# A decode block, forward and backward, on one core: the next step's key tile between two value tiles, a new order of every engine, and output rows in four column groups of TensorE

## Chip, core and metric

The kernel runs on one core of one Trainium2 chip. The core has five engines with their own instruction streams (TensorE, called PE; VectorE, DVE; ScalarE, ACT; GpSimd, POOL; SyncE, SP, which here only issues transfers) and 16 DMA engines that move data between HBM and the on-chip memory. The metric is the device time of one execution in microseconds, the median of several.

## What is computed

The reference computes a decode block with one new position per batch and then its whole gradient, for B = 2, D = 576, 32 query heads, 16 key heads, 4096 cached positions, head size 128 and a hidden size of 4608, all in bf16:

```python
xn = _layernorm(x)
y  = x + A(xn, k_cache, v_cache, wq, wo) + B(xn, w_gate, w_up, w_down)
# A: q = xn @ wq; p = softmax(q k^T / sqrt(128)); o = p v; o @ wo    (each key head serves two query heads)
# B: ((xn @ w_gate) * (xn @ w_up)) @ w_down
out, vjp = jax.vjp(f, x, k_cache, v_cache, wq, wo, w_gate, w_up, w_down)
return (out, *vjp(grad_out))
```

The outputs are out_0 (the block's output, 2 rows of 576), out_1 (the gradient of x, 2 rows), out_2 and out_3 (the gradients of the key and value cache, 2 x 16 x 4096 x 128 each), out_4 and out_5 (of wq and wo), out_6, out_7 and out_8 (of w_gate, w_up and w_down). The caches are read once (64 tiles of 1 MB) and gradients of the same size are written once (64 stores of 1 MB), and so are the weights: 92.48 MB in and 92.48 MB out.

## The kernel before

**Steps.** The attention goes in 16 steps s: eight groups of two key heads, for each of the two batches. A step loads two key tiles and two value tiles (128 x 4096 bf16, 1 MB, one for each head), and makes two 1 MB stores of dV (out_3, the softmax weights times the gradient of the head's output) and two of dK (out_2, the score gradients times q). The functions are `load_kv` (L1143) for the tiles, `softmax` (L1327), `dscore` (L1383), `contract` (L1434, products with a tile), and `head_outer` (L1287), whose matmuls L1299 build the blocks of dV and dK in PSUM. ACT (L470) or DVE (L472) copies each block of 128 x 1024 from PSUM into a bf16 tile, which is called an eviction here; after four of them `put` (L695) issues the store on SP (L699).

**Weights.** `load_w` (L1161) loads wq, wo, w_gate, w_up and w_down in between, and the MLP (`mlp`, L856) and the projections run among the attention's steps. The weights' gradients are outer products with few rows; `rows_outer`, `cols_outer`, `wide_outer` and `tail_outer` (L818) form them. `tail_outer` stores the last 64 rows of a gradient; some of these stores (the argument `few`) go out as 4 x 16 x 512 instead of 64 x 512.

**Buffers.** One ring of 16 tiles of 1 MB (`big`) serves key and value tiles, transposed tiles, gradients and weights, with a cap for each user. DVE transposes tiles at L466. SP issues 227 transfers between HBM and the on-chip memory (all but two small ones), in order, and each waits for the one eight before it.

**Who sets the order.** A class `Order` (L105 to L240) runs when the program is built. Each piece of the kernel is a generator that yields what it needs (an engine for so long, a buffer, a transfer, an event). The class keeps a model of when engines, buffers and transfers are free, and among the pieces that can go on an engine within `SLACK` of the first it picks the one of lowest priority value, `pr(name, s)` (L349): 28 for each step, and an offset from the tables `PR`, `HEAD`, `TAIL` and `OFF`. So the order of the instructions on every engine, SP included, is fixed in the program and comes out of these tables. `MLP_AT`, `WQ_AT` and `WO_AT` say when the weights are wanted.

**The last rows.** `final_out` (from L1502) adds x and the transposed sums to make out_0: two matmuls bring x (L1499), and 64-column matmuls with a unit matrix (L1513, L1516) add the sums, all on partitions 0 and 1. `final_dx` (from L1521) makes out_1: the norm's gradient on DVE (L1534 to L1545) and the same kind of transposing matmuls (L1549, L1552). In `rows_put` (L1489) ACT (L1491) and DVE (L1493) copy one part each into the tile `xy`, and SP stores it (L1495).

Of the kernel before, what the change touches and what calls it, by code (L numbers as in the profile page):

```python
# [104 lines left out]
class Order:  # L105
# [3 lines left out]
    def __init__(self):  # L109
        self.free = {e: 0.0 for e in ("PE", "ACT", "DVE", "POOL", "SP")}  # L110
        self.slots = {}
        self.home, self.cap, self.used = {}, {}, {}
        self.lines = Lines()
        self.quad, self.kind = (None, 0.0, 0.0), None
        self.streams = []
        self.count = 0
        self.log = []
        self.lanes = {"HW": [], "SW": []}
# [45 lines left out]
    def start(self, s):  # L164
# [30 lines left out]
    def run(self):  # L195
        while self.streams:
# [8 lines left out]
            if e is not None:  # L205
                t, _, s, e = min((c for c in cand if c[3] == e and c[0] <= t + SLACK[e]), key=lambda c: (c[1], c[0]))
# [27 lines left out]
            elif r[0] == "dma":  # L234
                self.free[e] = t + r[2]
# [55 lines left out]
def DMA(engine, cost, nbytes, row=8192):  # L291
    packet = 0.0364 * row + 8.7
    return ("dma", engine, cost, 0.02 + nbytes / 16e3 * packet / row, packet)

NBIG, NWW, NBD = 16, 5, 3
CAP = {"G": 2, "X": 10, "kv": 6, "st": 5}
OFF = {"turn0": {0: -1015.2, 1: -14.6, 2: -608.5, 3: -352.4, 4: -44.2, 5: -609.4, 6: 1026.5, 7: -575.3, 8: -336.9,
       9: -48.1, 10: 73.1, 12: 183.6, 13: 1140.9, 15: 354.0}, "turn1": {0: -158.8, 1: 373.8, 2: -399.3, 3: -123.5,  # L300
       4: -561.8, 5: 1792.7, 6: 184.6, 7: -225.4, 8: -1188.5, 9: -525.0, 10: -1211.4, 11: -134.5, 12: 1399.2, 13:
       -786.3, 14: 125.3, 15: -889.4}, "att": {0: -320.6, 1: 25.1, 2: -524.3, 3: 1437.6, 4: -1231.0, 5: 704.1, 6:
       -946.7, 7: -1656.2, 8: -1046.6, 9: 659.5, 10: -617.2, 11: -169.8, 12: 46.5, 13: -31.6, 14: -222.6, 15:
       1033.5}, "dsc": {0: -1811.3, 1: -9.9, 2: 131.1, 3: 301.3, 4: -3.2, 5: 235.2, 6: -975.3, 8: 26.8, 9: 229.2,
       10: -420.4, 11: 210.0, 12: 19.1, 13: 299.2, 14: 9.4}, "conv": {0: -2015.6, 1: 231.3, 2: -0.4, 3: -50.3, 4:
       -1165.8, 5: 1061.5, 6: 135.8, 7: 373.5, 8: -2359.6, 9: 3.5, 10: 1574.4, 11: 172.6, 12: 216.0, 13: 448.3, 14:
       255.6, 15: 10.6}, "con": {0: -32.2, 1: 1152.5, 2: 1696.5, 3: 720.8, 4: 638.1, 5: 104.8, 6: -260.9, 7: -158.3,
# [3 lines left out]
       9: -103.2, 10: -395.3, 11: 2850.9, 12: 125.0, 13: 2376.4, 15: -25.5}, "front": {0: -90.0, 1: 2844.9, 2:  # L311
       -805.5, 3: -966.7, 4: 1527.3, 5: 109.2, 6: 51.9, 7: -924.3, 8: -171.1, 9: -1466.9, 10: -796.2, 11: 95.0, 12:
       407.0, 13: 194.7, 14: 42.9, 15: -116.8}, "back": {0: -1180.5, 1: 591.1, 2: -2708.2, 3: 979.9, 4: 556.1, 5:
# [7 lines left out]
       13: -595.2, 14: -250.1, 15: 5.1}, "mlp": {0: 248.5, 1: 1168.1, 2: -620.3, 3: -398.1, 4: -321.8, 5: 2002.0, 6:  # L321
       162.1, 7: -3.7, 8: -33.1, 9: -2.4, 10: 1014.3, 11: 985.4, 12: 835.4, 13: -9.7, 14: 314.7, 15: -413.5},
       "load": {0: 1074.9, 1: -427.7, 2: 2940.0, 4: -302.0, 5: 501.3, 6: 157.2, 7: 2723.0, 8: 41.7, 9: 175.7, 10:
       -1207.2, 11: -514.7, 12: -5.8, 13: 248.9, 14: 607.8, 15: -253.7}, "wload": {0: -271.1, 1: 208.8, 2: -1828.2,
       3: 108.3, 4: 438.0, 5: -390.0, 6: 623.3, 7: 89.8, 8: -357.2, 9: -50.4, 10: 1806.6, 11: 48.4, 12: -1247.3, 13:
       3030.4, 14: 857.3, 15: 1037.7}, "mload": {0: 867.2, 1: -358.1, 2: -1319.2, 3: 100.2, 5: 58.5, 6: -3446.8, 9:
       -71.5, 10: -371.1, 11: -312.3, 12: 9.2, 13: 247.9, 14: 253.2, 15: -7.2}}
MLP_AT = [1.14, 5.4, 2.05, 2.45, 26.26, 69.69, 14.36, 0.0, 155.88]
WQ_AT = [-126, 9, 14, 22, -10, -36, 47, 13]
WO_AT = [-81, -88, -157, -95, 31, 1, -2, -56]  # L330
# [3 lines left out]
BIAS = 0.188  # L334
SLACK = {"PE": 0.06, "ACT": 0.25, "DVE": 0.4, "POOL": 10000.0, "SP": 10000.0}
STEP = 28.0
HEAD = {"turn0": -995.0, "turn1": -3790.2, "att": -3348.0, "dsc": 396.0, "conv": -832.5, "con": 1401.5, "out1":
        -1892.2, "out0": 2828.7, "front": 21.6, "back": 291.8, "W0": -1455.9, "W1": -155.0, "BD1": 1364.6, "BD0":
        2903.1, "mlp": 2389.4, "load": -3080.4, "wload": 394.7, "mload": -742.1}
TAIL = {"turn0": 3370.1, "turn1": 9221.8, "att": 665.4, "dsc": 359.0, "conv": 2694.5, "con": 2347.7, "out1": 7925.6,  # L340
        "out0": -1730.3, "front": 756.2, "back": 2986.8, "W0": 3398.4, "W1": -331.2, "BD1": -2581.8, "BD0": -508.7,
        "mlp": -5065.9, "load": 6824.2, "wload": 208.6, "mload": 3569.7}
PR = {"turn0": 1475.9, "turn1": 1614.7, "att": -4652.5, "dsc": -2890.4, "conv": 226.3, "con": -1413.1, "out1":
      3893.4, "out0": 2308.0, "front": 679.0, "back": 881.2, "W0": -1279.8, "W1": -624.6, "BD1": 2069.1, "BD0":
      -1551.4, "mlp": -735.6, "wout": -435.6, "store": -3305.7, "load": -1982.4, "wload": -3953.8, "fin": 5877.7,
      "const": 11595.3, "mload": -2275.6}
# [8 lines left out]
def kernel(  # L355
# [339 lines left out]
    def put(dst, src, nbytes, row, tag, slot, ready):  # L695
        yield WAIT(*ready)
        for d, x in zip(dst, src):
            yield DMA("SP", 0.36, nbytes, row)
# [119 lines left out]
    def tail_outer(rhss, dsts, p, event, w0=0, few=()):  # L818
# [5 lines left out]
        yield SPAWN(put(dsts, src, 64 * FS * 2, 1024, "tl", i, done), p + PR["store"])  # L824
# [31 lines left out]
    def mlp(i, hh, sl, Lgu, Ld, wd_slot):  # L856
# [36 lines left out]
        for k in range(NB):  # L893
            for e in range(2):
# [20 lines left out]
                               few=(0, 1) if i in FEW_M else (1,)), po)  # L915
# [136 lines left out]
    def group_back(g):  # L1052
# [13 lines left out]
        for t, x in ((0, R), (1, Q)):  # L1066
# [9 lines left out]
                               few=(0,) if g in FEW_G else ()), po)  # L1076
# [66 lines left out]
    def load_kv():  # L1143
        n = 0
        for s in range(NS):
            g, b = divmod(s, Bq)
            for t in range(2):
                for l in range(G):
                    yield PRIO(pr("load", s) if n else -1e5)
                    i = yield ACQ("kv")  # L1150
                    yield DMA("SP", 0.36, 1 << 20)
                    nc.sync.dma_start(kv_t[i][:], views[t][b, G * g + l])
                    kvS[s][t][l] = i
                    yield ("lset", kvL[s][t][l])
                    yield SET(issued[n])
                    n += 1
# [4 lines left out]
    def load_w(item):  # L1161
        kind, i = item
        if kind in ("wq", "wo"):
# [3 lines left out]
            if kind == "wq":  # L1167
# [5 lines left out]
                yield DMA("SP", 0.4, 128 * 4 * FS * 2, 1024)  # L1173
# [3 lines left out]
            else:  # L1177
                yield DMA("SP", 0.36, 128 * GH * D * 2, 4608)
# [3 lines left out]
        else:  # L1182
# [7 lines left out]
            for w, Wsrc in enumerate((B_w_gate, B_w_up)):  # L1190
                b = yield ACQ("G")
                sl["G"].append(b)
                yield DMA("SP", 0.4, 128 * 4 * width * 2, 2 * width)
# [9 lines left out]
            for hh, k in enumerate(ks):  # L1203
                d = yield ACQ("ww")
                Ld = Event()
                yield DMA("SP", 0.36, 128 * FC * D * 2, 4608)
# [282 lines left out]
    def rows_put(o, n, out):  # L1489
        yield ACT(0.4)  # L1490
        nc.scalar.copy(view(xy[:], 0, 2, n * D, [[P, 5], [1, 64]]), o[0:2, 0, 0:320].rearrange("p (k n) -> p k n", k=5))  # L1491
# [110 lines left out]
```

## Time and profile before

| | before |
|---|---|
| time, median of 3 runs | 463.32 us (462.25 to 463.77) |
| the profiled execution | 462.65 us, its span 460.7 us |
| mean granted TensorE clock | 0.721 |
| PE, DVE, ACT, POOL busy | 80%, 79%, 73%, 31% of the span |
| DMA | 185.97 MB, mean 404 GB/s |

The span is the time from the first to the last event of the execution in the profile; the execution's own time is some 2 us longer. The page cuts the span into 40 slices of 11.5 us and gives the busy share of each engine in tenths, and for the DMA engines the mean share of the 16 and the rate. Further views give the busy time in stretches of one's choice, the instructions of a stretch in order of time (the timeline), the chain of waits that ended last, and for each engine what its idle time ended with. SPq is SP's queue of transfers.

### The profile page before, as it was taken

How to read it: one execution, taken by the hardware profiler on the slowest of the kernel's cores; microseconds unless marked ns; L12 is line 12 of the kernel's file. 1: busy time of each engine (PE TensorE's matmuls, PEld its weight loads, DVE VectorE, ACT ScalarE, POOL GpSimd, SP SyncE). 2: the span in 40 equal slices, each digit the busy share in tenths (PEclk: the TensorE clock that was granted, in tenths of full speed). 3: DMA queues.
4: the chain of work that ended last, by engine and by line, in shares of the span. 5: the costliest groups of instructions: out<-in, count | busy, mean ns of one | idle time of the engine just before them, and what ended most of it. 6: DMA issues, size and time to landing. Idle time of an engine off the chain costs nothing.

```text
span 460.7 us, 15711 instructions
## 1 busy us (share of the span) xinstructions
PE 369.5 (80%) x6750; PEld 214.3 (47%) x6750; DVE 365.9 (79%) x708; ACT 336.8 (73%) x516; POOL 143.4 (31%) x174
## 2 busy tenths in 40 slices
PE   1688879798986786896978897877988887987994
PEld 1445456555443343554546364544444542544453
DVE  8887888896789687878887679886976987887782
ACT  4269638878986586775767859867867997897973
POOL 0740043403407341660016151050164364063000
PEclk9967676888776667757685678877567676675856
DMA  8999999999999999999999999999999999999995
GB/s 316 413 408 422 410 423 400 410 415 398 373 424 421 408 422 410 421 419 413 413 403 417 417 418 419 422 418 388 398 423 417 418 423 426 423 409 392 421 346 209
DMA packets 40494, 185.97 MB, mean 404 GB/s; under 512 B 3424, under 2 KB 12136, under 8 KB 24040
## 3 DMA queue, kind: packets, MB, share of 16 engines
q1 hardware_dynamic: 40416, 184.96, 99.0%
q8 instruction: 53, 0.87, 0.7%
q14 instruction: 17, 0.14, 0.1%
q10 hardware_dynamic: 8, 0.00, 0.0%
HBM read 92.48 MB, written 92.48 MB: 401 GB/s over the span
## 4 chain that ended last, share of the span: by engine, by line
DMA 34%; PE 30%; ACT 14%; DVE 12%; issue 5%; SPq 3%; DVEq 0%; ACTq 0%
DMA big<-in_A_v_cache_dram 15%; DMA out_dram<-big 14%; ACT big L470 12%; DVE big L466 7%; PE ps_o L1299 5%; PE ps_m L1451 4%; PE ps_o L730 4%; PE ps_m L1277 4%; DMA big<-in_A_k_cache_dram 3%; SPq L1201 2%; PE ps_o L767 2%; DVE big L472 2%; PE ps_m L895 2%; PE ps_m L681 2%; DMA ww<-in_A_wq_dram 1%
## 5 line engine op out<-in xcount | busy, mean ns | idle before, releaser
L470 ACT CAST big<-ps_o 128x1024 bf16<-128x1024 f32 (+2 forms) x309 | 278.9, 964 | 49.8 <-PE ps_o L1299 24.3
L466 DVE STREAM_TRANSPOSE big<-big 128x1024 f32<-128x1024 f32 x146 | 176.3, 1222 | 16.1 <-DMA big<-in_A_v_cache_dram 6.3
L1265 POOL TENSOR_TENSOR BD<-vr,mask 128x2048 bf16<-128x2048 bf16 x32 | 115.3, 3604 | 114.3 <-DVE vr L472 45.4
L472 DVE CAST big<-ps_o 128x1024 bf16<-128x1024 f32 (+1 forms) x69 | 73.4, 1065 | 19.4 <-PE ps_o L767 6.1
L1277 PE MATMUL ps_m<-big,W 128*32 128x128 bf16 x2048 | 59.7, 280 | 4.5 <-issue 1.7
L1242 POOL COPY W<-rep 32x16 bf16<-32x16 bf16 x128 | 24.8, 193 | 117.9 <-DVE rep L1015 102.0
L1277 PEld LDWEIGHTS <-W 128*32 128x32 bf16 x2048 | 47.2, 125 | 25.1 <-issue 23.9
L1299 PE MATMUL ps_o<-BD,dd 32*128 32x512 bf16 x256 | 46.9, 497 | 9.1 <-ACT big L470 8.1
L1299 PE MATMUL ps_o<-BD,pp 32*128 32x512 bf16 x256 | 44.6, 473 | 8.9 <-ACT big L470 7.3
L466 DVE STREAM_TRANSPOSE big<-ww 128x1152 f32<-128x1152 f32 (+1 forms) x25 | 32.9, 1318 | 2.6 <-DMA out_dram<-big 2.5
L1451 PE MATMUL ps_m<-big,pp 128*32 128x512 bf16 x256 | 28.9, 540 | 4.1 <-DVE pp L466 2.4
L1451 PE MATMUL ps_m<-big,dd 128*32 128x512 bf16 x256 | 27.8, 528 | 1.7 <-DVE dd L466 0.6
L1299 PEld LDWEIGHTS <-dd 32*128 32x128 bf16 x256 | 11.2, 98 | 26.5 <-issue 20.0
L1299 PEld LDWEIGHTS <-pp 32*128 32x128 bf16 x256 | 10.3, 95 | 28.1 <-issue 24.5
L767 PEld LDWEIGHTS <-xnr 32*128 32x128 bf16 x368 | 13.1, 114 | 14.5 <-issue 13.1
L730 PE MATMUL ps_o<-dyr,R 32*32 32x288 bf16 x256 | 17.8, 401 | 1.2 <-ACT big L470 1.1
L767 PE MATMUL ps_o<-D,xnr 32*128 32x128 bf16 x256 | 13.9, 265 | 5.7 <-ACT big L470 4.3
L730 PE MATMUL ps_o<-dyr,hb 32*32 32x288 bf16 x288 | 15.7, 328 | 2.8 <-ACT big L470 2.7
L1047 POOL COPY qr<-qd 128x256 bf16<-128x256 bf16 x8 | 3.2, 398 | 47.4 <-DVE qd L472 43.2
L895 PE MATMUL ps_m<-big,Wdy 128*128 128x128 bf16 x162 | 16.7, 285 | 0.6 <-DVE cr L1403 0.5
L895 PEld LDWEIGHTS <-Wdy 128*128 128x128 bf16 x162 | 15.1, 131 | 2.9 <-issue 2.7
L1352 ACT COPY mr<-m 1x128 f32<-1x128 f32 x16 | 4.7, 295 | 15.1 <-DVE m L1350 14.9
(210 smaller groups left out, 488.2 us busy)
## 6 DMA issues: line engine op xcount, KB each, us to landing
out_dram<-big SPq DMA_DIRECT2D x74, 1024.0 KB
big<-in_A_k_cache_dram SPq DMA_DIRECT2D x32, 1024.0 KB
big<-in_A_v_cache_dram SPq DMA_DIRECT2D x32, 1024.0 KB
out_dram<-big SPq DMA_DIRECT2D x17, 576.0 KB
ww<-in_B_w_down_dram SPq DMA_DIRECT2D x9, 576.0 KB
ww<-in_A_wo_dram SPq DMA_DIRECT2D x8, 576.0 KB
ww<-in_A_wq_dram SPq DMA_DIRECT2D x8, 512.0 KB
big<-in_B_w_gate_dram SPq DMA_DIRECT2D x4, 1024.0 KB
```

Source lines behind the costliest of these rows:

```text
L466: nc.vector.transpose(out, in_)
L470: nc.scalar.copy(out, in_)
L472: nc.vector.tensor_copy(out=out, in_=in_)
L681: nc.tensor.matmul(dp[32 * q:32 * q + 32, 0:P], lhsT=W, rhs=view(X, 0, P, xoff(q, s), [[FS, 4], [2, 32]]), start=(s == 0), stop=(s == S - 1))
L730: nc.tensor.matmul(o[32 * q:32 * q + 32, aa, 0:HD2], lhsT=view(t, 32 * q, 32, 2 * A + aa, [[4, 32]]), rhs=dyr[32 * q:32 * q + 32, k * HD2: ...
L767: nc.tensor.matmul(o[:, aa, j * P:(j + 1) * P], lhsT=xnr[32 * a:32 * a + 32, dc * P:(dc + 1) * P], rhs=rhs(a), start=True, stop=True)
L895: nc.tensor.matmul(dh, lhsT=Wdy[:, e, 2 * k:2 * k + P], rhs=view(X[:], 0, P, 64 * k + e, [[D, FC], [2, 32]]), start=(k == 0 and e == 0), s ...
L1242: nc.gpsimd.tensor_copy(view(W_t[t][w][:], 32 * a, 32, 6 + 8 * a, [[G * WW, 4], [WW, G], [1, 2]]), view(rep_t[grp[g]["qs"]][:], 32 * a, 32 ...
L1265: nc.gpsimd.tensor_tensor(BD_t[i][:], view(vr_t[v][:], 0, P, 0, [[0, 16], [1, Dh]]), view(mask16[:], 0, P, 0, [[1, 16], [0, Dh]]), ALU.mult)
L1277: nc.tensor.matmul(sc[32 * cq:32 * cq + 32, :], lhsT=view(W[:], 0, P, (be * G + l) * WW + 6 - 4 * c2 - 2 * l, [[1, 32]]), rhs=view(X[:], 0 ...
L1299: nc.tensor.matmul(o[:, k, :], lhsT=pr2[32 * c4:32 * c4 + 32, :], rhs=BD[32 * c4:32 * c4 + 32, 8 * l + 4 * h2:8 * l + 4 * h2 + 4, :], star ...
L1451: nc.tensor.matmul(ct[32 * j:32 * j + 32, :], lhsT=view(rT, 0, P, 4 * c + 2 * l, [[1, 32]]), rhs=kv_t[kvS[s][t][l]][:, Dh * c:Dh * (c + 4) ...
```

## The change

Three things change.

1. `load_kv` no longer loads a step's four tiles together. The order of the tiles is k0 k1 v0 | k0' v1 k1' v0' | k0'' v1' ...: the first key tile of the next step stands between the two value tiles of a step.
2. The planner knows kinds of transfers: 1 is a big load, 2 a store of over 500,000 bytes. After a big load it puts another big load 0.67 us later in its model (`NEAR`), and, if a load would be the best next transfer, takes a store instead whose priority value is within `APART` of the load's. All tables of priorities, `SLACK`, `BIAS` and the times of the weights have new values, so that the order of every engine is another. `few` becomes a table of how many engines a tail store uses, which the planner doesn't read further; the transfers stay.
3. The last rows are formed in four column groups of PE: each piece of 128 columns of the output row stands on partitions 32q and 32q + 1 of PSUM. The copies out of PSUM are then one for each group: two on ACT and two (out_0) or three (out_1) on DVE.

```diff
@@ Order.start
         if r[0] == "dma":
             lanes = self.lanes["SW" if r[1] == "POOL" else "HW"]
-            return max([s.ready, self.free[r[1]]] + [when(x) for x in lanes[-8:-7]]), r[1]
+            t = max([s.ready, self.free[r[1]]] + [when(x) for x in lanes[-8:-7]])
+            return t + NEAR if r[5] == self.moved == 1 else t, r[1]
@@ Order.run
             if e is not None:
-                t, _, s, e = min((c for c in cand if c[3] == e and c[0] <= t + SLACK[e]), key=lambda c: (c[1], c[0]))
+                cand = [c for c in cand if c[3] == e and c[0] <= t + SLACK[e]]
+                best = min(cand, key=lambda c: (c[1], c[0]))
+                if e == "SP" and best[2].req[5] == self.moved == 1:
+                    best = min((c for c in cand if c[2].req[5] == 2 and c[1][0] <= best[1][0] + APART),
+                               key=lambda c: (c[1], c[0]), default=best)
+                t, _, s, e = best
@@ tables
+APART, NEAR = 12697.9, 0.67
...
-BIAS = 0.188
-SLACK = {"PE": 0.06, "ACT": 0.25, "DVE": 0.4, "POOL": 10000.0, "SP": 10000.0}
+BIAS = 0.313
+SLACK = {"PE": 0.1, "ACT": 0.16, "DVE": 0.5, "POOL": 10000.0, "SP": 10000.0}
...
@@ load_kv
-        n = 0
-        for s in range(NS):
+        order = sorted(((s, t, l) for s in range(NS) for t in range(2) for l in range(G)),
+                       key=lambda x: 4 * x[0] + 3.5 * x[1] + x[2])
+        for n, (s, t, l) in enumerate(order):
             g, b = divmod(s, Bq)
...
-                    yield DMA("SP", 0.36, 1 << 20)
+            yield DMA("SP", 0.36, 1 << 20, 8192, 1)
...
@@ final_out
-        rows_add(o, 0)
-        for dc in range(5):
-            r = slice(0, P) if dc < 4 else slice(64, P)
-            for k in range(2):
-                if dc < 4:
-                    nc.tensor.matmul(o[0:2, k, 64 * dc:64 * dc + 64], lhsT=acc[:, dc, :],
-                                     rhs=identf[:, 64 * k:64 * k + 64], start=False, stop=(dc == 3 and k == 1))
...
+        for q in range(4):
+            w = P if q < 3 else P + 64
+            nc.tensor.matmul(o[32 * q:32 * q + 2, 0, 0:w], lhsT=ident[0:2, 0:2], rhs=xy[:, P * q:P * q + w],
+                             start=True, stop=False)
+        for q in range(4):
+            nc.tensor.matmul(o[32 * q:32 * q + 2, 0, 0:P], lhsT=acc[:, q, :], rhs=identf[:], start=False, stop=(q < 3))
...
-        yield from rows_put(o, 0, out_0)
+        yield from rows_put(o, 0, out_0, [([[1, P + 64]], 384, (96, 0)), ([[1, P]], 256, (64, 0)),
+                                          ([[1, P]], 0, (0, 0)), ([[1, P]], P, (32, 0))])
@@ final_dx
         for a in range(4):
-            nc.tensor.matmul(view(o[:], 0, 2, 512 * (a // 2) + 32 * (a % 2), [[64, 4], [1, 32]]),
-                             lhsT=gx[:, 2 * a:2 * a + 2], rhs=identf[:], start=False, stop=(a == 3))
+            nc.tensor.matmul(o[32 * a:32 * a + 2, 0, 0:P], lhsT=gx[:, 2 * a:2 * a + 2], rhs=identf[:],
+                             start=False, stop=True)
```

More of the change, by code (lines that the diff above doesn't have):

```diff
@@ L116, in __init__ @@
         self.count = 0
+        self.moved = None
         self.log = []
@@ L234, in run @@
             elif r[0] == "dma":
+                self.moved = r[5] or self.moved
                 self.free[e] = t + r[2]
@@ L693, in tail_at, with put @@
         return h, c < FT, c if c < FT else c - FT
-    def put(dst, src, nbytes, row, tag, slot, ready):
+    def put(dst, src, nbytes, row, tag, slot, ready, few={}):
         yield WAIT(*ready)
-        for d, x in zip(dst, src):
-            yield DMA("SP", 0.36, nbytes, row)
+        for k, (d, x) in enumerate(zip(dst, src)):
+            yield DMA("SP", 0.36, nbytes, row, 2 if nbytes > 500000 else 0, few.get(k, 16))
             nc.sync.dma_start(d, x)
@@ L823, in tail_outer @@
         dsts = [d.rearrange("(r q) f -> q r f", q=4) if k in few else d for k, d in enumerate(dsts)]
-        yield SPAWN(put(dsts, src, 64 * FS * 2, 1024, "tl", i, done), p + PR["store"])
+        yield SPAWN(put(dsts, src, 64 * FS * 2, 1024, "tl", i, done, few), p + PR["store"])
         def mk(A):
@@ L1487, in fronts, with rows_put, copies @@
             yield from group_front(g)
-    def rows_put(o, n, out):
+    def rows_put(o, n, out, parts):
+        def copies(eng, some):
+            for dims, r, c0 in some:
+                dst, src = view(xy[:], 0, 2, n * D + r, dims), view(o[:], c0[0], 2, c0[1], [[1, dims[0][1] * (dims[1][1] if len(dims) > 1 else 1)]])
+                if len(dims) > 1:
+                    src = src.rearrange("p (c i) -> p c i", i=dims[1][1])
+                cp(eng, dst, src)
         yield ACT(0.4)
-        nc.scalar.copy(view(xy[:], 0, 2, n * D, [[P, 5], [1, 64]]), o[0:2, 0, 0:320].rearrange("p (k n) -> p k n", k=5))
+        copies("ACT", parts[:2])
         yield DVE(0.4)
-        nc.vector.tensor_copy(view(xy[:], 0, 2, n * D + 64, [[P, 4], [1, 64]]), o[0:2, 1, 0:256].rearrange("p (k n) -> p k n", k=4))
+        copies("DVE", parts[2:])
         yield DMA("SP", 0.3, 2304, 1152)
         nc.sync.dma_start(out.rearrange("b s d -> (b s) d"), xy[:, n * D:(n + 1) * D])
-    def rows_add(o, n):
-        for k in range(2):
-            nc.tensor.matmul(o[0:2, k, 0:320 - 64 * k], lhsT=ident[0:2, 0:2],
-                             rhs=view(xy[:], 0, 2, n * D + 64 * k, [[P, 5 - k], [1, 64]]), start=True, stop=False)
     def final_out():
@@ L1531, in final_dx @@
         nc.tensor.matmul(mt[0:16, 8:16], lhsT=accx[:, P:144], rhs=F8[:], start=True, stop=True)
-        rows_add(o, 1)
+        for a in range(4):
+            nc.tensor.matmul(o[32 * a:32 * a + 2, 0, 0:P], lhsT=ident[0:2, 0:2],
+                             rhs=view(xy[:], 0, 2, D + 32 * a, [[P, 4], [1, 32]]), start=True, stop=False)
+        nc.tensor.matmul(o[96:98, 1, 0:64], lhsT=ident[0:2, 0:2], rhs=xy[:, D + 512:2 * D], start=True, stop=False)
         yield DVE(0.5)
```

107 lines of the change are left out of this document (51 added, 56 removed), and 20 rows, old and new, of the table OFF.

## The prediction

> **What bounds the kernel now.** I read the page's slices first, then its queues.
>
> ```profile
> DMA  8999999999999999999999999999999999999995
> GB/s 316 413 408 422 410 423 400 410 415 398 373 424 421 408 422 410 421 419 413 413 403 417 417 418 419 422 418 388 398 423 417 418 423 426 423 409 392 421 346 209
> ...
> q1 hardware_dynamic: 40416, 184.96, 99.0%
> ```
>
> The 16 DMA engines are at 9 tenths or more in 38 of 40 slices, and one queue's 184.96 MB take 99.0% of their time. Room shows in the first slice and the last, and the rate drops in the last two. I therefore asked for the busy time in chosen stretches (DMA share and GB/s are the last two columns; some stretches overlap).
>
> ```profile
> 0.00:30.67 30.67, 15.45 (x251) 9.85 (x252) 26.68 (x92) 11.25 (x23) 14.91 (x26) 0.89 0.96 374
> 30.67:442.00 411.33, 341.33 (x6277) 196.39 (x6276) 331.09 (x596) 316.80 (x482) 128.45 (x148) 0.71 1.02 413
> 115.20:126.70 11.50, 10.65 (x203) 5.68 (x202) 8.48 (x15) 11.10 (x16) 4.89 (x8) 0.74 1.00 372
> 126.70:311.00 184.30, 150.38 (x2757) 88.65 (x2757) 150.87 (x273) 132.81 (x202) 62.92 (x76) 0.70 1.02 416
> 311.00:322.50 11.50, 8.48 (x172) 5.09 (x171) 7.55 (x12) 8.54 (x13) 0.00 (x0) 0.70 1.00 388
> 414.60:426.10 11.50, 8.83 (x138) 4.67 (x133) 8.50 (x16) 8.51 (x14) 3.60 (x1) 0.50 1.02 391
> 442.00:446.00 4.00, 3.95 (x105) 2.59 (x106) 2.83 (x6) 3.55 (x5) 0.00 (x0) 0.50 0.71 242
> 446.00:450.00 4.00, 4.00 (x64) 2.53 (x60) 2.85 (x5) 1.56 (x4) 0.00 (x0) 0.63 1.04 402
> 448.00:452.00 4.00, 3.64 (x80) 2.60 (x77) 1.91 (x7) 2.62 (x5) 0.00 (x0) 0.88 0.96 390
> 450.00:456.00 6.00, 4.66 (x76) 3.00 (x61) 2.08 (x11) 3.22 (x5) 0.00 (x0) 0.70 0.84 316
> 456.00:460.70 4.70, 0.12 (x5) 0.00 (x0) 0.34 (x1) 0.41 (x1) 0.00 (x0) 0.50 0.10 36
> ```
>
> From 30.67 to 442 us the DMA share is 1.02: over 411 us no order of the compute engines can make the transfers start sooner in sum, and only their rate (413 GB/s) can move. It does move: 372, 388 and 391 GB/s in three stretches, at shares of 1.00 to 1.02. So those stretches are slow transfers, not missing ones. Room is left in 442 to 446 (0.71) and 450 to 456 (0.84). What happens at the very end is in the DMA part for 452 to 460.7, whose 40 slices are 0.22 us each:
>
> ```profile
> DMA  9999944634179989992111211111111100000000
> GB/s 377 431 419 435 393 137 158 181 129 167 64 278 391 377 287 348 386 311 85 71 66 57 85 42 41 49 47 47 47 52 47 47 28 24 0 0 0 0 0 0
> ```
>
> From slice 19 (about 456.1) the share is one or two tenths, 1.6 to 3.2 engines of 16, at a steady 47 GB/s. That goes on to about 459.2 (slice 33). Fourteen or so engines are done at 456.1 and about two are still working off a backlog for 3 us. Their share never falls to 0 in the starved slices before either (the lowest is a 1). The end at 460.7 is then the last landing of what these two carry, 1.5 us after their last bytes. I infer two lagging engines from shares; the view doesn't name them. The Trainium skill, page "DMA: Bandwidth & Descriptors", section "Latency and other measured facts", says that two of the 16 DMA engines are usually slower in traces; the tail of one to two tenths agrees with two.
>
> The compute side of the end:
>
> ```profile
> 449.70 0.27 SPq L1495 DMA_DIRECT2D out_dram<-xy  x1
> 450.85 0.35 SPq L699 DMA_DIRECT2D out_dram<-big  x1
> 451.31 1.08 SPq L699 DMA_DIRECT2D out_dram<-tl  x1
> 453.47 0.38 SPq L699 DMA_DIRECT2D out_dram<-big  x1
> 456.59 0.26 SPq L1495 DMA_DIRECT2D out_dram<-xy  x1
> ```
>
> ```profile
> 450.85 0.37 ACT L470 CAST tl<-ps_o 64x256 bf16<-64x256 f32 x1
> 451.31 2.13 ACT L470 CAST big<-ps_o 128x1024 bf16<-128x1024 f32 x2
> 456.15 0.41 ACT L1491 CAST xy<-ps_o 2x320 bf16<-2x320 f32 x1 [2.71 <-PE ps_o L1552]
> ```
>
> ```profile
> 453.95 1.87 PE ps_o L1549 x8
> 455.82 0.31 PE ps_o L1552 x8
> ```
>
> The chain of waits ends in PE's L1549 and L1552, then ACT's copy of the row, then the issue of out_1 at 456.59. That looks like a compute chain that sets the end. But out_1 is 2 KB, and the slices show two engines busy with older bytes until 459.2.
>
> **Load order.** Nothing is removed: the same 64 key and value tiles and the same 227 transfers stand in SP's order after, with the same bytes. In step 0, v1 comes one tile later (1 MB at 413 GB/s: 2.5 us), and gate and up come two tiles later.
>
> ```profile
> 30.67 5.04 SPq L699 DMA_DIRECT2D out_dram<-big  x2
> ```
>
> The first store stands behind the same loads as before, 8 tiles of 1.05 MB and 5.4 MB of weights, 13.8 MB. In the trace it goes out at 30.67. By then 30.67 us x 374 GB/s = 11.5 MB have moved, so 2.3 MB, 5.6 us, are still in front of it. That covers the 2.5 us; without cover it would cost 2.5 us less whatever remained. I take 0. At the other end the last key tiles come one place earlier and the last value tiles hardly move. The order after has 13.4 MB behind its last load (w_down), as before: ten stores of 1.05 MB, two of 0.59, three of 0.52 and three tails of 0.07.
>
> **Alternation of loads and stores.** The planner now prefers a store of over 0.5 MB right after a load. Counted in SP's order over transfers of 0.45 MB and more, loads and stores form 78 runs after and 76 before: the alternation hardly changes. What a change of direction costs is not shown by a row; the bounds are the three slow stretches. Against 416 GB/s they lose 11.5 x (1 − 372/416) = 1.2 us, 0.8 us and 0.7 us. All of them gone is −2.7 us; twice as many is +2.7 us. I take 0, since the 76 and 78 runs give no reason for either.
>
> **New engine orders.** The work is the same, so in the covered 411 us their cost is 0 as long as SP isn't held up for longer than its queued transfers last. SP does wait for evictions:
>
> ```profile
> SPq L699 <- ACT big L470: 86.7, 55, 4.7
> SPq L699 <- DVE big L472: 63.9, 28, 5.6
> ```
>
> Waits of up to 5.6 us left the share at 1.02. Up to 8 transfers are out at once (each waits for the one 8 before it), about 20 us at 2.5 us per MB. A wait of 5.6 us would have to become several times longer, with all that stands behind it in SP's order, loads and stores alike, to let the DMA engines run dry. I take 0, and keep a stall of one wait, +3 us, as an upper end.
>
> In the tail I counted ACT's evictions behind the last load in both orders:
>
> ```profile
> L470 ACT CAST big<-ps_o 128x1024 bf16<-128x1024 f32 x26 | 25.0, 1027 | 1.8 <-PE ps_o L1299 1.6
> L470 ACT CAST big<-ps_o 128x576 bf16<-128x576 f32 x5 | 3.1, 644 | 0.3 <-PE ps_o L730 0.3
> ```
>
> Before: 33 evictions of 1024 columns and 5 of 576, 33 x 1.027 + 5 x 0.644 = 37.1 us. After: 32 and 7, 37.4 us. That is 0.3 us more, nothing to speak of. What differs is the last piece. Before, the last big store is 512 KB, evicted by 453.44 (451.31 + 2.13). After, a 1 MB store of dV follows it, and ACT evicts two more blocks in front of the last row's copies: 2 x 1.03 = 2.05 us, so ACT is done at about 455.5. Before, ACT stood idle for 2.71 us in that place, so the copies wait no longer. The 1 MB goes out at 455.5 and takes 2.5 us on engines that are free: 458.0, ahead of the 459.2 at which the two late engines finish. The bytes in all are the same for these two. So 0, with 1.2 us of cover: past 459.2 − 2.5 = 456.7 each us of delay of that eviction is a us of time.
>
> **Column groups.** The matmuls of out_0 in the trace, beside L1549's above:
>
> ```profile
> 447.16 1.87 PE L1513 MATMUL ps_o<-identf,acc 128*2 128x64 f32 x16
> ```
>
> In out_0, 16 records of matmuls with 64 columns (1.87 us) become 8 with 128 columns over four groups; in out_1 the 8 remain, and go to four groups.
>
> If four groups run at once, L1549's 1.87 us become 0.47, −1.4; if not at all, 0. The copies grow from one per engine (0.41 us) to two on ACT and three on DVE, at most ACT's 0.41 us each: up to +0.8 us. So the issue at 456.59 moves between −1.4 and +0.8, and the likely value, near the gain, is −0.6 or better. On the time it is worth 0, because the late engines end at 459.2 whichever it is. The Trainium skill, page "TensorEngine Tiling (Array Packing)", section "Key Properties", says that different tiles run loads and matmuls in parallel; by it the sum would take the full −1.4 on the chain, and no row here shows four groups at this shape.
>
> **The sum.** 0 + 0 + 0 + 0 against the profiled execution, 462.65 us (span 460.7). The three timed runs have 463.32 in the middle, 462.25 to 463.77; the mean of all four is 463.0, which I take for the changed kernel.
>
> **The rivals.**
>
> *Tail filled, faster.* The new order keeps the engines supplied in 442 to 446 and 450 to 456. Against the share of 1.03 of a full stretch, (1.03 − 0.71) x 4 = 1.3 us and (1.03 − 0.84) x 6 = 1.1 us come free: 463.0 − 2.4 = 460.6. For it: the last key tiles come earlier against the bytes behind them, and PE's short chain of the end. Against it: the two late engines never ran dry in those slices, so filling the other 14 moves nothing.
>
> *The chain of the row sets the end, faster.* If 460.7 was out_1's own landing (4.1 us after 456.59), and not the late engines, then the groups' −1.4 shows in full: 461.6. For it is the chain of waits, which ends there; against it are the slices at 47 GB/s up to 459.2. The Trainium skill, page "DMA: Bandwidth & Descriptors", section "Anatomy of one DMA", gives about 2 us for the fixed cost of a transfer; an estimate from it, 456.59 + 0.26 + 2 = 458.9, would leave the end to the late engines.
>
> *The last 1 MB store comes late, slower.* In 442 to 450 PE is busy 7.95 of 8 us, at a granted clock of 0.50 and 0.63: PE sets the pace of the evictions there. In 448 to 452 the clock was 0.88. If the clock of the new order stays at 0.50 there, the 3.64 us become 6.4, +2.8 us, and the last eviction moves from 455.5 to 458.3. That is 1.6 past the point of 456.7: 463.0 + 1.6 = 464.6. One more slow stretch on top, 1.2, makes 465.8. For it: a 1 MB store now stands last, where 512 KB stood. Against it: ACT's work is equal, and 1.2 us of cover.
>
> *SP held up in the body, slower.* One wait at SP beyond the cover: +3 us, 466.0. Nothing in the trace is near it.
>
> *The change doesn't do what it says.* 78 runs against 76 say that the alternation is not really there; the time is then that of the forecast, which stands on this already.
>
> **How the numbers follow.** Two executions of this kernel differ by up to 0.3% (1.5 us), so that much, about 1.4 us, is what a measurement can tell from no change. No change 0.39; tail filled 0.23; chain of the row 0.10, of which −1.4 lies at the very bound; last store late 0.21; SP held up 0.07. Faster transfers in the body go with the tail's gain, slower ones with the late store. So faster 0.33, same 0.39, slower 0.28. The range goes from the filled tail with one slow stretch less, 460.6 − 1.2, to the late store with one more, 465.8: 459.4 to 465.8. The likeliest case's own range is 461.6 to 464.4. Time 463.0 us.
>
> **What would show it right or wrong.** Right: DMA share of 1.0 or more from 12 to 440, about 413 GB/s over the body, a tail of one to two tenths of DMA share for some 2 to 3 us after the last big store, an issue of out_1 at or before 456.6, and L1513's and L1549's successors well below 1.87 us. The first rival shows as shares of 1.0 up to the last stores and an end some 2 us earlier. The third shows as a last eviction behind 456.7 and all 16 engines busy after it. A body rate off 413 GB/s by 0.5% is 2 us, and would make the forecast wrong for a reason that none of these steps can size.

## The result, and the profile after

| | before | changed |
|---|---|---|
| median | 463.54 us (4 runs, 462.25 to 463.86) | 477.10 us (4 runs, 475.42 to 482.36) |
| ratio to before, 95% interval | 1 | 1.0317 [1.0231, 1.0403] |
| the profiled execution, its span | 462.65, 460.7 us | 478.22, 476.4 us |

The change makes the kernel slower by 3.2%, 13.6 us between the medians. The forecast was 463.0, with a range up to 465.8. The page of the changed kernel, in its slices of 11.9 us:

```profile
DMA  8999999999999998797999999999989999989996
GB/s 322 421 399 428 411 418 400 419 424 418 418 407 411 414 424 344 311 389 267 377 340 414 421 423 418 422 405 407 408 334 357 421 418 398 422 339 372 424 411 238
...
q1 hardware_dynamic: 40416, 184.96, 96.8%
```

The packets and the bytes are the same. What changed is inside the body, which the forecast had called covered. The slices with a share under 9 tenths, 15, 16, 18, 29 and 35, move 344, 311, 267, 334 and 339 GB/s. Slice 20 moves 340 at a share of 9 tenths or more: there the transfers themselves were slow. The queue's share gives a split of the 15.7 us that the span grew. Its transfers took 0.968 x 476.4 = 461.2 us, before 0.990 x 460.7 = 456.1: 5.1 us more for the same packets. The rest of the span, in which the engines had nothing from this queue, grew from 4.6 to 15.2 us: 10.6 us. A full stretch for comparison, then the worst stretches one by one (the last two columns are DMA share and GB/s):

```profile
60.00:180.00 120.00, 101.21 (x1931) 59.77 (x1924) 95.84 (x177) 93.36 (x150) 42.75 (x60) 0.73 1.02 416
178.00:188.00 10.00, 0.59 (x1) 0.14 (x2) 2.42 (x3) 0.77 (x2) 0.00 (x0) 0.50 0.98 410
187.00:192.00 5.00, 3.90 (x65) 1.78 (x68) 0.42 (x1) 1.66 (x3) 0.00 (x0) 0.50 0.31 128
...
222.00:226.00 4.00, 3.21 (x21) 0.65 (x20) 2.82 (x6) 2.83 (x6) 0.00 (x0) 0.50 0.31 127
344.00:350.00 6.00, 5.89 (x73) 3.49 (x69) 4.92 (x6) 5.27 (x10) 1.53 (x8) 0.50 0.68 257
416.00:420.00 4.00, 3.74 (x80) 2.12 (x77) 2.63 (x5) 4.00 (x7) 3.32 (x1) 0.71 0.66 274
```

From 60 to 180 us the changed kernel runs at 1.02, like before. Then comes a stretch of 10 us in which the DMA engines are full but PE works 0.59 us, DVE 2.42 and ACT 0.77. After it the DMA engines are empty as well (0.31). The compute engines stopped first, the transfers afterwards. What the compute engines waited for stands in the timelines of PE, ACT and SP around that place:

```profile
178.34 0.59 PE L1458 MATMUL ps_m<-big,pp 128*32 128x512 bf16 x1 [0.60 <-ACT big L479]
188.10 1.04 PE L1458 MATMUL ps_m<-big,pp 128*32 128x512 bf16 x7 [9.17 <-DMA big<-in_A_v_cache_dram]
```

```profile
189.79 1.18 ACT L479 CAST big<-ps_o 128x576 bf16<-128x576 f32 x2 [11.02 <-PE ps_o L739]
```

```profile
172.97 0.34 SPq L1160 DMA_DIRECT2D big<-in_A_v_cache_dram  x1
173.40 0.43 SPq L1160 DMA_DIRECT2D big<-in_A_k_cache_dram  x1
176.54 0.33 SPq L1214 DMA_DIRECT2D ww<-in_B_w_down_dram  x1
191.00 0.34 SPq L708 DMA_DIRECT2D out_dram<-big  x1
```

L1458 (L1451 before) is the product of the softmax weights with the value tiles in `contract`. Its matmuls read v0 and v1 in turn. In step 6 the first one runs on v0 at 178.34. The second reads v1, and PE sits for 9.17 us until v1 lands. SP issued v1 at 172.97. The place that v1 gave up to the next step's key tile k0' (163.67 in SP's timeline) lies 9.3 us earlier. PE works in order, so the matmuls behind it stand, and ACT has nothing to evict for 11.02 us. SP's next entry is a store that needs such an eviction; it stands from 176.9 to 191.0, and the loads behind that store stand too. The transfers already issued last until about 187, then the DMA engines run dry.

The stretch from 344 to 350 has the same start: PE waits 4.71 us for v1, until 340.93. No wait for v1 stands at the product ahead of the other two, 222 to 226 and 416 to 420. There SP stands with a row of stores (three in 211.53 to 224.79, four in 409.32 to 419.99) that wait for their evictions; they come up again under "What stays".

The views of waits count both kinds for the whole run (the total in us, how often, the longest), for SP and for PE:

```profile
SPq L708 <- ACT big L479: 137.6, 61, 14.0
```

```profile
PE ps_m L1458 <- DMA big<-in_A_v_cache_dram: 17.3, 5, 9.2
```

Before, SP's longest wait for ACT was 4.7 us (for DVE 5.6), and no wait of PE for a value transfer stood at the product.

Why is PE put there too early? The planner's `contract` is started when the softmax is done, and in the planner it doesn't ask whether v0 and v1 have landed; only DVE's transposes of the same tiles ask (L1230 in the changed kernel). In the old order of loads the two value tiles come directly behind the key tiles that the softmax needs. Adding the missing wait to the program of before leaves every instruction of every engine in its place: in that plan it never binds. With k0' ahead of v1, it binds (the run planner_waits_v below), and the planner of the changed kernel doesn't know. That is **theory A**: PE is put in front of a product whose tile hasn't landed, and what stands behind it stops. Its rival, **theory B**: the new tables as such put stores too early in SP's order, wherever the value tile is.

### The profile page after: what moved, and what is told of

It is laid out like the page before. It is cut to its first block, busy times and chain, and to the rows that moved or that the text cites. A ratio compares the mean times of both kernels' runs of the same rounds, so it can differ in the third digit from the quotient of the medians.

```text
span 476.4 us, 15736 instructions
## 1 busy us (share of the span) xinstructions
PE 372.9 (78%) x6747; PEld 215.3 (45%) x6747; DVE 354.4 (74%) x687; ACT 347.1 (73%) x542; POOL 143.3 (30%) x174
## 4 chain that ended last, share of the span: by engine, by line
PE 38%; DMA 29%; ACT 16%; DVE 9%; issue 4%; SPq 1%; ACTq 0%; DVEq 0%
DMA big<-in_A_v_cache_dram 17%; ACT big L479 14%; DMA out_dram<-big 9%; PE ps_m L1458 7%; PE ps_o L1306 7%; DVE big L475 5%; PE ps_m L1284 5%; PE ps_o L739 4%; DMA big<-in_B_w_up_dram 3%; PE ps_m L1040 2%; PE ps_m L904 2%; PE ps_m L886 1%; SPq L1208 1%; PE ps_o L776 1%; PE ps_m L690 1%
## 5 line engine op out<-in xcount | busy, mean ns | idle before, releaser
L479 ACT CAST big<-ps_o 128x1024 bf16<-128x1024 f32 (+2 forms) x322 | 286.0, 959 | 44.2 <-PE ps_o L739 19.9
L475 DVE STREAM_TRANSPOSE big<-big 128x1024 f32<-128x1024 f32 x146 | 175.4, 1221 | 15.7 <-DMA big<-in_A_v_cache_dram 5.8
L481 DVE CAST big<-ps_o 128x1024 bf16<-128x1024 f32 (+1 forms) x56 | 63.0, 1126 | 6.8 <-PE ps_o L1306 3.8
L1284 PE MATMUL ps_m<-big,W 128*32 128x128 bf16 x2048 | 56.8, 269 | 2.0 <-issue 1.2
L1306 PE MATMUL ps_o<-BD,pp 32*128 32x512 bf16 x256 | 47.2, 484 | 11.0 <-ACT big L479 10.1
L1306 PE MATMUL ps_o<-BD,dd 32*128 32x512 bf16 x256 | 46.8, 489 | 10.6 <-ACT big L479 8.1
L1284 PEld LDWEIGHTS <-W 128*32 128x32 bf16 x2048 | 44.7, 120 | 20.3 <-issue 18.4
L1458 PE MATMUL ps_m<-big,pp 128*32 128x512 bf16 x256 | 31.3, 540 | 19.3 <-DMA big<-in_A_v_cache_dram 17.3
L1458 PE MATMUL ps_m<-big,dd 128*32 128x512 bf16 x256 | 29.2, 550 | 1.5 <-DVE D L912 1.1
L1458 PEld LDWEIGHTS <-pp 128*32 128x32 bf16 x256 | 5.9, 108 | 28.9 <-issue 25.2
L479 ACT CAST tl<-ps_o 128x256 bf16<-128x256 f32 (+1 forms) x28 | 9.8, 376 | 11.8 <-PE ps_o L840 11.6
L690 PE MATMUL ps_m<-big,wm 128*32 128x128 bf16 x416 | 13.9, 292 | 3.8 <-DVE big L475 2.8
L739 PE MATMUL ps_o<-dyr,R 32*32 32x288 bf16 x256 | 15.7, 373 | 1.3 <-ACT big L479 1.0
L1468 ACT ACTIVATE osb<-ps_m 128x512 bf16<-128x512 f32 x16 | 9.8, 612 | 8.4 <-PE ps_m L1458 7.0
## 6 DMA issues: line engine op xcount, KB each, us to landing
big<-in_A_k_cache_dram SPq DMA_DIRECT2D x32, 1024.0 KB, 10.6
ww<-in_B_w_down_dram SPq DMA_DIRECT2D x9, 576.0 KB, 10.8
ww<-in_A_wo_dram SPq DMA_DIRECT2D x8, 576.0 KB, 10.6
```

Of the source, the lines that this page charges most:

```text
L475: nc.vector.transpose(out, in_)
L479: nc.scalar.copy(out, in_)
L481: nc.vector.tensor_copy(out=out, in_=in_)
L690: nc.tensor.matmul(dp[32 * q:32 * q + 32, 0:P], lhsT=W, rhs=view(X, 0, P, xoff(q, s), [[FS, 4], [2, 32]]), start=(s == 0), stop=(s == S - 1))
L739: nc.tensor.matmul(o[32 * q:32 * q + 32, aa, 0:HD2], lhsT=view(t, 32 * q, 32, 2 * A + aa, [[4, 32]]), rhs=dyr[32 * q:32 * q + 32, k * HD2: ...
L1284: nc.tensor.matmul(sc[32 * cq:32 * cq + 32, :], lhsT=view(W[:], 0, P, (be * G + l) * WW + 6 - 4 * c2 - 2 * l, [[1, 32]]), rhs=view(X[:], 0 ...
```

## Experiments

All ratios are against runs of the kernel before on the same chip (medians 463.3 to 463.7). Line numbers move a little with each edit: the product is L1451 before, L1458 in the changed kernel, and up to three lines off in a variant.

### The wait alone taken away, in both kernels

```diff
-                                     rhs=kv_t[kvS[s][t][l]][:, Dh * c:Dh * (c + 4)],
+                                     rhs=kv_t[kvS[s][t][0 if t else l]][:, Dh * c:Dh * (c + 4)],
```

In the changed kernel:

> The changed kernel with one index changed: in the product of the softmax weights with the values, both halves read the first value tile, so the output rows use v0 where v1 belongs. The order of every engine stays that of the changed kernel; only PE no longer waits for v1's transfer. Theory A (PE, in order, is put in front of a product whose second value tile has not landed, and everything queued behind it stops until SP and the DMA engines run dry): PE's wait for the value transfer at the product falls from 17.3 us to under 5 us, SP's longest wait for an eviction from 14.0 to about 6 us, no stretch of 12 us between 60 and 430 us has a DMA share under 0.9, and the time falls by 9 to 14 us, to 463 to 468 us. Theory B (the new tables as such, with stores that SP must issue before their evictions are done, hold SP up wherever the value tile is): PE's wait goes, but SP's waits for ACT stay near 137.6 us and the time stays within 3 us of 477.

Measured: 466.26 us, 1.006 [1.0035, 1.0085]. That is 10.8 us less than the changed kernel, with the same instructions in the same order. The product reads v0 in v1's place. In the view of the product's waits the value transfer no longer appears, and the queue's share is back:

```profile
q1 hardware_dynamic: 40416, 184.96, 98.7%
```

SP's waits for ACT only fell to 125.6 us (longest 8.3), yet the time fell: their sum was never the measure, the long ones were. Theory A's price is right; two details missed. SP's longest wait stayed at 8.3, not 6, and one stretch of 12 us (around 216) had a share of 0.86. The edit does one thing more: v1's tile comes free without the product, and SP's loads waited 8.3 us for that product instead of 12.2. The exchange of loads below leaves the product as it is, and so is free of that.

The control, the same edit in the kernel before:

> The kernel before with the same index changed as in v1_not_awaited: the product reads the first value tile twice, so the output rows use v0 where v1 belongs. The order of every engine stays that of before. Theory A: in before v1 has always landed when PE comes to the product (no wait for a value transfer stands there), so the time stays within 0.4% of before, 461.7 to 465.4. Were the gain of v1_not_awaited one of leaving the tile out as such (a tile that comes free earlier), it would show here too: 2 us less or more.

Measured: 463.59 us, 1.0002 [0.9984, 1.002]. Leaving the tile out is worth nothing in an order in which it has always landed.

### Loads exchanged, with every engine's order held

Both kernels let one test the load order without planning anew: the places of SP's loads stay, and only which of two tiles is loaded in a place is exchanged. PE, DVE, ACT and POOL keep their instructions in order.

```diff
+    EARLY = (2, 3, 6, 8, 11, 12, 13, 14)
...
-            nc.sync.dma_start(kv_t[i][:], views[t][b, G * g + l])
-            kvS[s][t][l] = i
+            x = (s - 1, 1, 1) if s - 1 in EARLY and t + l == 0 else (s + 1, 0, 0) if s in EARLY and t and l else (s, t, l)
+            nc.sync.dma_start(kv_t[i][:], views[x[1]][x[0] % Bq, G * (x[0] // Bq) + x[2]])
+            kvS[x[0]][x[1]][x[2]] = i
```

> The changed kernel with the transfers of v1 and of the next step's first key tile exchanged back in eight steps (2, 3, 6, 8, 11, 12, 13, 14), the planner not told: every engine keeps the order of the changed kernel, and only eight pairs of loads on SP change places. The program computes the whole reference. Theory A: PE's waits for v1 at the product (9.2, 4.7 and 2.2 us in steps 6, 11 and 12) fall by the two or three transfers by which v1 now comes earlier, to under 8 us in all; the key tile comes later, for which DVE's transposes may wait up to 10 us in all, in an order in which DVE has little else to do. Time 466 to 474 us, against 477. Theory B (tables): 476 to 479.

Measured: 468.30 us (466.73 to 469.09), 1.0096 [1.0062, 1.013]. Eight pairs of loads in their old order give 8.8 of the 13.6 us back, with the new tables and engine orders untouched. In stretches of 4 us from 12 to 440, those behind a wait for v1 are full again; under 0.9 are only 220 to 224 (0.70) and 404 to 412 (0.82 and 0.85). The views of waits of PE and DVE:

```profile
PE ps_m L1461 <- DMA big<-in_A_v_cache_dram: 3.2, 2, 2.3
```

```profile
DVE big L475 <- DMA big<-in_A_v_cache_dram: 9.2, 5, 2.3
```

PE's 17.3 us became 3.2. The key tiles that come later in exchange show no cost: no wait of PE or DVE for a key transfer stands in the views.

The other way round, in the kernel before, v1 and k0' change places in seven steps (`LATE = (0, 2, 6, 7, 9, 12, 14)`, the same kind of edit):

> The kernel before, with the transfers of v1 and of the next step's first key tile exchanged in seven steps (0, 2, 6, 7, 9, 12, 14), and the planner not told: every engine keeps the order of before, only seven pairs of loads on SP change places. Theory A (PE meets the product ahead of v1's landing, because the planner lets the product start without asking for the value tiles): waits for the value transfer appear at PE's product or at DVE's transposes, over 8 us in all (before: 0 at the product, 6.3 at the transposes), and the time rises by 4 to 20 us, to 467 to 484. Theory B (what costs is the new tables): within 2 us of before.

Measured: 469.30 us (468.0 to 469.66), 1.0121 [1.0104, 1.0137], 6.0 us more. Waits for the value tiles appear where there were few:

```profile
PE ps_m L1454 <- DMA big<-in_A_v_cache_dram: 9.9, 3, 4.4
```

```profile
DVE big L466 <- DMA big<-in_A_v_cache_dram: 18.9, 8, 6.5
```

With the index changed on top:

> v1_later with the index changed as in v1_not_awaited: the product reads the first value tile twice, so the output rows use v0 where v1 belongs. Theory A: most of what v1_later lost comes back if the loss is at PE's product; what stays is lost at DVE's transposes of the late tiles, which are still waited for. 463 to 470 us, and under half of v1_later's loss.

Measured: 467.70 us, 1.0085 [1.006, 1.011]. Here I was wrong: only 1.6 of the 6.0 us came back (and the single times of the two runs overlap), and over half stayed. What stayed goes with DVE's transposes, whose waits for the value tiles are 21.9 us in this run; that they are its cause isn't shown, since no run takes them away. So a late v1 is dear in both orders, but in the old one not mainly through the product.

### One part of the change alone, or taken out

The load order alone, in the kernel before with its own tables (`load_kv` as in the change, no rule):

> The kernel before with only the new order of the key and value loads, its own tables and no rule of the planner. Theory A: the value tile v1 comes 2 transfers later, PE waits for it at the product (before: 0 us; here over 10 us), and SP and the DMA engines run dry after those waits; 470 to 490 us. Theory B: the load order is harmless, what costs is the new tables; within 4 us of before, 460 to 467.

Measured: 496.92 us, 1.0728 [1.0692, 1.0763], above A's range; PE's waits for the value transfer at the product came to 24.7 us. With the index changed in it:

> load_order_alone (496.92 us) with the same index changed: the product reads the first value tile twice. The engine orders are those of load_order_alone. Theory A: PE's wait for the value transfer (24.7 us in all at the product) falls to under 8 us, and the time falls by 8 to 16 us, to 481 to 489 us; the rest, some 20 us over before, is that the old tables put SP's stores and loads in an order that doesn't suit these loads. Theory B: within 3 us of 497.

Measured: 480.22 us, 1.0356 [1.032, 1.0392]: 16.7 us less, a little above what was expected. Leaving v1 out is worth half of the 33.3 us that the load order costs here. The other 16.6 us are not split further: the old tables, replayed with these loads, give another order of everything.

The changed kernel with the old load order:

> The changed kernel with the loads of a step in the order of before (k0 k1 v0 v1); tables, rule and column groups are the new ones, and the engine orders come out anew. Theory A: PE's wait for the value transfer at the product goes (under 2 us of 17.3). The time is open, since the tables were found for the other order: A only says that what is lost then is lost at other waits (SP for evictions), 465 to 490 us. If PE's wait at the product stays above 8 us, the load order is not its cause.

Measured: 479.17 us, 1.0347 [1.0296, 1.0398]. PE's wait for the value transfer at the product is 1.9 us of 17.3, and the time is no better. With these tables the old load order loses as much by other waits, as theory A allowed for; it comes with another order of every engine, from tables that were made for the other loads. So the time of this run speaks neither for A nor against it; PE's wait, which goes with the old order, speaks for A.

The changed kernel without the planner's rule (both conditions on `self.moved` off):

> The changed kernel without the planner's rule that prefers a store after a load; tables, load order and column groups stay, the engine orders come out anew. Theory A: the product is still planned without asking for v1, so PE's waits for the value transfer stay, over 8 us in all, and the time is no better than 477, up to 500. If the rule is the cause, the time falls toward 464.

Measured: 493.73 us, 1.0649 [1.0631, 1.0667]; PE's wait for the value transfer is 19.0 us in 7 places. So PE's wait doesn't need the rule. What it is worth can't be read from this, for the reason above.

### The planner told of the wait

```diff
-        yield WAIT(Ezero, grp[g]["EoT"])
+        yield WAIT(Ezero, grp[g]["EoT"], *kvL[s][t])
```

> The changed kernel with one wait added in the planner: the product with the value tiles waits for both tiles' landing in the planner's model, as the transposes do already. The program computes the same; the engine orders come out anew, with tables that were not found for it. Theory A: PE's wait for the value transfer at the product falls to under 4 us of 17.3, since the planner puts other work in front; but the tables are not made for it, so the time may stay at 472 to 482 us, with the idle time moved to other waits. If the blind product were no cause, the wait at the product would stay as it is.

Measured: 480.68 us, 1.0393 [1.0339, 1.0446]. PE's wait at the product falls from 17.3 to 1.6 us, SP's waits for DVE's evictions grow from 44.9 to 77.8 us, and those for ACT's fall from 137.6 to 110.6. Once the planner sees the landing, it moves the product behind it, but with these tables no time is gained.

### The end of the run

The kernel before with the column groups alone (`rows_put`, `final_out` and `final_dx` as in the change):

> The kernel before with only the output rows in four column groups. The prediction's step: the chain of the last row gets shorter by 1.2 to 1.4 us (1.87 to about 0.6 us for its matmuls), out_1 is issued earlier, and the time stays within 0.3% of before (462.0 to 464.9), because two late DMA engines end the run. The rival of the prediction: the row's own landing sets the end, and the time falls by 1.0 to 1.4 us.

Measured: 464.00 us over 10 runs, 1.0008 [0.9993, 1.0023]. But out_1 was issued at 456.53, no earlier than before (456.59), so this run doesn't test what sets the end. The kernel before with out_1 not waiting for its chain:

```diff
-        nc.scalar.copy(view(xy[:], 0, 2, n * D, [[P, 5], [1, 64]]), ...
+        nc.scalar.copy(view(xy[:], 0, 2, 0, [[P, 5], [1, 64]]), ...
-        nc.vector.tensor_copy(view(xy[:], 0, 2, n * D + 64, [[P, 4], [1, 64]]), ...
+        nc.vector.tensor_copy(view(xy[:], 0, 2, 64, [[P, 4], [1, 64]]), ...
```

> The kernel before, with out_1 stored from the part of the tile that holds grad_out since the start, so that SP doesn't wait for the last row's chain; the copies of the last row go to the other part and are not stored. The order of every engine is that of before. The prediction's reading (two late DMA engines end the run): out_1 is issued about 2.7 us earlier, near 453.9, and the time stays within 0.3% of before, 462.2 to 465.0. The rival (the row's own landing ends the run): 1.3 to 2.7 us less, 460.9 to 462.3.

Measured: 463.99 us over 10 runs, 1.0014 [0.9997, 1.0031]. In its timeline out_1 follows the last big store directly, where before it came 3.1 us after it:

```profile
455.45 0.39 SPq L699 DMA_DIRECT2D out_dram<-big  x1
455.89 0.35 SPq L1495 DMA_DIRECT2D out_dram<-xy  x1
```

SP no longer waits for the chain, and over ten runs there is no gain, where the rival asked for 1.3 to 2.7 us: this is against the row's chain as what sets the end of before. One detail missed: in the profiled execution out_1 went out at 455.89, not near 453.9, because the last big store itself came 2.0 us later than in the profile of before (455.45 against 453.47). Whether the edit delays that store or this execution did can't be told from one profile. In groups_alone the last DMA slices (452.0 to 461.4, 0.235 us each) have the same tail as before:

```profile
DMA  9899957444349989991310101111111110000000
GB/s 390 360 449 414 458 229 283 166 163 176 137 159 381 405 301 379 379 353 65 126 63 39 69 39 59 41 46 46 52 44 52 44 52 31 0 0 0 0 0 0
```

## Why the prediction was wrong

**Load order: the step that failed.** The prediction followed the moved tiles to the first store of the run and to the last load, and took 0. It never asked who reads v1 first, and in which engine's order that reader stands. Its "v1 comes one tile later" was right for step 0; in step 6 it was 9.3 us. What it left out is that the reader is PE's product, in order, with evictions and through them SP's stores behind it. The exchange of eight pairs of loads shows the size of this term: 8.8 us, where the sum had 0.

**New engine orders: a term mis-sized.** The prediction named the mechanism (SP held up beyond its cover, with loads behind the stores) but gave it +3 us and a chance of 0.07, since it took 5.6 us for the longest wait and put the cover at 20 us. (SP's longest wait of before was 8.7 us, for PE ahead of a load of w_down, and it left the DMA share full too.) The cover was about half of that. After SP's last issue at 176.54 the engines were dry from 187 on, 10.5 us later. At some 420 GB/s that is 4.4 MB, less than SP's last five transfers (4.8 MB): eight is a limit that SP, held up by evictions, hadn't reached. The wait was 14.0 us. Without v1's wait the longest for an eviction was 8.3.

**What stays.** Without the wait for v1 2.7 us of loss remain (466.26 against 463.60). Part of it is the two stretches with no wait for v1 ahead of them, which come back shorter. The trace of v1_not_awaited shows 1.8 us of empty share in 216 to 220 and 1.0 us in 404 to 408:

```profile
216.00:220.00 4.00, 3.00 (x33) 0.71 (x21) 2.79 (x7) 3.07 (x6) 0.00 (x0) 0.50 0.58 237
404.00:408.00 4.00, 2.99 (x99) 2.10 (x95) 3.16 (x5) 4.00 (x8) 3.60 (x1) 1.00 0.76 317
```

Before the first of them SP stands with three stores for 12.75 us (206.58 to 219.33) ahead of the next value load; a row of shorter waits lets the engines run dry as well:

```profile
206.58 12.75 SPq L708 DMA_DIRECT2D out_dram<-big  x3
219.43 0.37 SPq L1160 DMA_DIRECT2D big<-in_A_v_cache_dram  x1
```

That is theory B's share, in a small size; I only read it from the trace and didn't take it away. Why the same packets took 5.1 us longer in the changed kernel isn't settled either; in v1_not_awaited they took 0.987 x 464.3 = 458.3 us, 2.2 more than before. In before_v1_not_awaited, whose order is that of before, they took 0.988 x 463.2 = 457.6, so some 1.5 us of this can be chance.

**Alternation.** The prediction took 0 because it counted 78 runs of loads and stores after and 76 before. Counted again in SP's timelines, over the same transfers, it is 78 before and 90 after: the alternation does rise, and neither the 0 nor the rival "doesn't do what it says" had that ground. A price for it doesn't show: 60 to 180 us of the changed kernel move 416 GB/s at a full share, as 126.7 to 311 did before. No run separates it: with the rule off the order is another one as a whole.

**Column groups: right in the time, not in the copies.** L1513 and L1549 took 1.87 us each; their successors in the changed kernel:

```profile
462.05 0.61 PE L1522 MATMUL ps_o<-identf,acc 128*2 128x128 f32 x8
468.59 0.61 PE L1559 MATMUL ps_o<-identf,gg 128*2 128x128 f32 x8
```

That is 0.61 us against an estimate of 0.47 for four groups at once. The statement of the Trainium skill, page "TensorEngine Tiling (Array Packing)", section "Key Properties", that tiles run in parallel agrees with the 0.61 us. In groups_alone the time didn't move, as predicted, but in part by luck: the gain of 1.26 us, of which 0.6 or more was expected to be left, didn't even reach the issue of out_1 (456.53 in groups_alone, 456.59 before), because the copies took it back: in groups_alone DVE's three start only when ACT's two are done.

```profile
455.65 0.81 DVE L472 CAST xy<-ps_o 2x128 bf16<-2x128 f32 x3 [1.56 <-ACT xy L470]
```

**The end set by late DMA engines: not refuted for before, hardly there after.** With out_1 not waiting for the chain the time of before stayed, which speaks against the chain; that late engines set the end, and that they are two, is still an inference from shares of one to two tenths at about 47 GB/s. The Trainium skill, page "DMA: Bandwidth & Descriptors", section "Latency and other measured facts", speaks of two slower engines, but calls the effect specific to the path on which GpSimd issues transfers; here the data went by SP's hardware queue (q1), so the page doesn't explain this tail. The fixed cost of 2 us that the prediction took from the Trainium skill, same page, section "Anatomy of one DMA", was measured on that path too; no run here shows it alone. In the changed kernel the forecast's 2 to 3 us of such a tail didn't come. The slices of 462.0 to 476.4, 0.36 us each, are full almost until the bytes end, with two of them at one to three tenths, 0.7 us:

```profile
DMA  9999999976899973333799979999989310000000
GB/s 390 410 383 390 394 363 363 346 256 219 326 418 401 401 258 142 134 125 126 257 364 356 346 245 373 464 492 481 375 364 387 137 49 23 23 3 0 0 0 0
```

**The last 1 MB store late.** This rival's signs were there, a last eviction behind 456.7 and the engines busy after it: in v1_not_awaited the last big store goes out at 458.98, where the prediction had 455.5 for it, in a span that is 3.6 us longer as a whole. What it costs alone wasn't tried.

## What to carry to other kernels

For each transfer that a change moves, find its first reader on every engine that works in order, and what is queued behind that reader; a busy DMA view says nothing on how much slack the reader has. In a planner, let each piece wait for all the tiles that it reads, even where the order of the day makes a wait needless: a later change of that order turns the gap into a stall that the plan doesn't show. (Putting the wait in afterwards, with tables made without it, gained nothing here.) And where an order comes out of tables, undoing one part and planning again measures the tables; exchange two transfers with every other instruction held, and the part is measured.

## What was not expected of the hardware

A wait of 9.2 us on PE held SP for 14.0 us, and the DMA engines, full when PE stopped, fell to a share of 0.31 from 187 to 192. Transfers in flight hid the first 8 us of the stall, from 179 to 187, and nothing after them.
